# Other places and other turns for the sums of w1's blocks in a fused HGRN2 and mixer kernel

## The chip, the cores and the metric

The kernel runs on one core of a Trainium2 chip. The metric is device time in microseconds (us) for one execution, and the median of several executions stands for a kernel. Times within an execution come from one profiled execution and are counted from the start of its span. The engines are called as the profile calls them: PE is TensorE, DVE is VectorE, ACT is ScalarE, POOL is GpSimd, SP is SyncE.

## The reference, cut to what matters

Two blocks follow each other. The first is a gated recurrence for each of 4 batches and 8 heads, over 768 steps, with a state of 48 x 48. Its output, with the heads side by side, is the input `x` of the second, a mixer: a low-rank mixing along the sequence, and a two-layer channel network with a residual.

```python
# q, k, v, f_logit: (4, 8, 768, 48)
f = 1.0 / (1.0 + np.exp(-f_logit))
for t in range(S):
    state = f[:, :, t, :, None] * state + np.einsum('bhd,bhe->bhde', k[:, :, t], v[:, :, t])
    y[:, :, t] = np.einsum('bhd,bhde->bhe', q[:, :, t], state)
# x: (4, 768, 384), the heads of y side by side
# U: (768, 32), V: (32, 768), w_ch1: (384, 1536), w_ch2: (1536, 384)
h = xt @ U @ V                      # xt = x.transpose(0, 2, 1)
u = x + h.transpose(0, 2, 1)
ch = np.maximum(u @ w_ch1, 0.0) @ w_ch2
return u + ch
```

## The kernel before

**Attention.** The sequence is cut into chunks of 64 steps, and two heads are handled together; such a pair is a unit, and there are 16 units, 4 for each batch. The gates' products within a chunk are scanned on VectorE (`keep`, L827, backwards, into row 4 of the tile `late`; `read`, L845, forwards, into row 5). For a unit TensorE then makes the scores `sc` (L923), the transposed keys `pt` (L950), the chunks' states `ds` (L971), and the output `y` in two parts: from the states (L1009) and from the masked scores (L1027). VectorE multiplies `sc` by the causal mask into `A` (L936) and scans the states into `added` (L993); GpSimd copies them into `st` (L997), which the first part of `y` reads. ScalarE copies `ds` into `added` (L978), `pt` into `kb` (L954) and `y` into `x` (L1033), and spreads the chunks' whole gates into `whole` (L960).

**Mixer.** For each batch, `low_rank`, `added_up` and `mix` (`ph`, `pu`) add the mixing to `x`; `turn` transposes it into `uT` (`put`); `first` multiplies by `w1` (`pz`, L279) with a relu on ScalarE into `z_all` (L314); and the second layer is done by `seven` in four steps of `pw` products (L365), with sums `S` of z blocks (tiles `w_raw`, four additions of `sums_of`). A sequence block `a` is 256 rows; a batch has three. The tile `z_all` has 18 columns of 256 and is used as three thirds of 6 columns.

**The last blocks.** From batch 2's second block on, the first layer is done by `fewer` with 15 products of 128 x 512 instead of the plain ones (`pp`, L468). For that it needs sums of blocks of `x` (`sums_of_x`) and 14 sums of blocks of `w1`, 128 x 512 each. `W_SUMS` lists these: `(9, 0, '+', 1)` makes node 9 from nodes 0 and 1; nodes below 9 are blocks of `w1` itself. `w_node` looks up where a node lies, through `W_PLACES`, an index into the list `w_places`: ten pieces of `late` (0 to 9), the two tiles `fz` (10 and 11), and `added` (12). Those tiles serve the attention too, so a sum can be written only when attention no longer needs its place. `places_of_x` lists the places of the x sums: three `v_nat` tiles and two `st` tiles, of four pieces each, in that order.

**Order of the work.** The order on TensorE is the order of the program. In the second half of the kernel VectorE and ScalarE get theirs from a scheduler by priority; operations in `add` and the mask have a high one. `steps` yields the attention's pieces, `attention` runs them, and `Fill` puts the mixer's products between them. The 14 sums are called from `beside` in the last stretch of attention (the units of batch 3, beside block 0 of batch 2's mixer): one after each piece from piece 16 on.

```python
pieces = beside(steps((B - 1) * HP + 1, NU + 1), 10 * (HP - 2) - 4, [lambda i=i: sum_of_w(i) for i in range(len(W_SUMS))])
todo = m.first(0) + m.ready(0) + m.halved(0)
attention(pieces, Fill(todo[:-1], 33))
```

Just ahead of it stands `start_mixer(2, after)`: the mixing of batch 2 between the four steps of `seven` for batch 1's last block.

Of the kernel before, what the change touches and what calls it, by code (L numbers as in the profile page):

```python
# [39 lines left out]
W_SUMS = (  # L40
    (9, 0, '+', 1), (10, 4, '+', 9), (11, 5, '-', 10), (12, 2, '+', 11), (13, 4, '-', 5), (14, 4, '+', 7),
    (15, 6, '+', 14), (16, 5, '-', 15), (17, 8, '+', 16), (18, 6, '+', 17), (19, 3, '+', 15), (20, 0, '-', 18),
    (21, 0, '+', 14), (22, 2, '+', 20),
)
W_PLACES = (0, 1, 2, 3, 4, 5, 6, 7, 8, 9, 10, 11, 5, 12)
PRODUCTS = (
    ((2, 17),), ((7, 18),), ((11, 20),), ((6, 21),), ((13, 0),), ((1, 3),), ((8, 15),), ((4, 19),),
    ((9, 10),), ((10, 16),), ((3, 22),), ((12, 11),), ((0, 12),), ((15, 13),), ((14, 9),),
# [489 lines left out]
def factored_path(ctx, tc, q, k, v, f_logit, moe_U, moe_V, moe_w_ch1, moe_w_ch2, out, ok):  # L538
# [5 lines left out]
    B, H, S, D = q.shape  # L544
    P = nc.NUM_PARTITIONS
    C = P // 2
    NCH = S // C

    NBL = S // P
    HP = H // 2  # L550
# [4 lines left out]
    NFC = FF // P  # L555
    NU = B * HP
# [25 lines left out]
    z_all = const.tile([P, 3 * NFC // 2, 2 * P], F32, name="z_all")  # L582
# [20 lines left out]
    def load(n, *names):  # L603

        b, hp = divmod(n, HP)
        for nm in names:
            if nm == "v":
                v_tiles[n] = three.tile([P, NBL, 2, D], F32, name="v_nat")
            for par in range(2):
                head = src[nm][b, 2 * hp + par]  # L610
                if nm in "kq" and n < HP:
                    if par == 0:
                        nc.sync.dma_start(
                            out=packed(n, nm).rearrange("p (h t) -> p h t", h=2),
                            in_=src[nm][b, 2 * hp : 2 * hp + 2].rearrange("h (p c) d -> p h (c d)", p=P),
                        )
                    continue
                if nm == "v" and par:

                    for s in range(2):  # L620
                        nc.sync.dma_start(
                            out=v_tiles[n][(1 - s) * C : (2 - s) * C, :, par, :],
                            in_=head.rearrange("(c s p) d -> s p c d", s=2, p=C)[s],
                        )
                    continue
                if nm == "v" or n < TURNED:
                    dst = v_tiles[n] if nm == "v" else nat[n % 2][nm]
                    nc.sync.dma_start(out=dst[:, :, par, 0:D], in_=head.rearrange("(c p) d -> p c d", p=P))
                    continue
                head = head.rearrange("(c i) d -> i c d", i=NB)  # L630
                for part in range(2):
                    p0 = par * PAD + part * NB
                    n_ch = min(NB, D - part * NB)
                    nc.sync.dma_start(
                        out=raw[n % 2][nm][p0 : p0 + NB, :].rearrange("p (c d) -> p c d", d=NB)[:, :, 0:n_ch],
                        in_=head[:, :, part * NB : part * NB + n_ch],
                    )
# [225 lines left out]
    FG = FF // 3  # L863
    w_places, x_places, v_places, room = [], [], [], {}

    def w_node(n):
        if n < 9:
            return w1[:, n // 3, n % 3 * FG : (n % 3 + 1) * FG]
        return w_places[W_PLACES[n - 9]]

    def sum_of_w(i):
        if i == 0:
            flat = late.rearrange("p a s -> p (a s)")
            w_places.extend(flat[:, j * FG : (j + 1) * FG] for j in range(7 * S // FG))
            w_places.extend(t[:, 0:FG] for t in fz + [added])
            assert max(W_PLACES) < len(w_places)
        n, p, sign, q = W_SUMS[i]
        nc.vector.tensor_tensor(w_node(n), w_node(p), w_node(q), ALU.add if sign == "+" else ALU.subtract)

    def places_of_x():  # L880
        if not x_places:
            some = [three.tile([P, NBL, 2, D], F32, name="v_nat").rearrange("p c h d -> p (c h d)") for _ in range(3)]
            some += [two.tile([P, NCH, D], F32, name="st").rearrange("p c d -> p (c d)") for _ in range(2)]
            x_places.extend(t[:, i * P : (i + 1) * P] for t in some for i in range(NCH * D // P))
        return x_places

    def places_of_values():
# [155 lines left out]
    def front(n, *names):  # L1043

        if n >= NU:
            return []
        if n not in ahead:
            names_of = ("gates", "keep", "keys", "read_back", "queries", "gates_end", "unpack_k", "unpack_q")
            ahead[n] = dict(zip(names_of, prepare(n)))
        return [ahead[n].pop(nm) for nm in names if nm in ahead[n]]  # L1050

    def rear(n, *names):

        if not 0 <= n < NU:
            return []
        if n not in here:
            here[n] = dict(zip(("kept", "states", "scan", "scores", "read", "inner", "mask", "spread"), attend(n)))
        return [here[n].pop(nm) for nm in names if nm in here[n]]

    def joined(*groups):  # L1060

        groups = [g for g in groups if g]
        for _ in groups[1:]:
            yield lambda: None
        if groups:
            yield lambda: [f() for g in groups for f in g]

    def steps(first, last):

        def behind(n):  # L1070

            return HP + 3 <= n < NU - 1

        for n in range(first, last):
            if n < NU:
                yield from joined(rear(n - 2, "inner"), rear(n - 1, "scores"), rear(n, "kept"))
            else:
                for piece in rear(n - 2, "inner") + rear(n - 1, "scores"):
                    yield lambda: None
                    yield piece  # L1080
            if behind(n):
                yield from front(n, "read_back", "queries")
            if n + 1 < NU and n + 1 not in v_tiles:
                load(n + 1, "v")
            yield from front(n + 1, "gates", "keep", "keys")
            yield from joined(rear(n - 1, "read"), rear(n, "states", "scan"))
            if not behind(n + 1):
                yield from front(n + 1, "read_back", "queries")
            if n + 1 == last:
                yield from rear(n - 1, "inner")  # L1090
                if n + 2 < NU:
                    load(n + 2, "v")
# [5 lines left out]
            piece()  # L1098
        fill.rest()

    def beside(pieces, n, calls):

        for i, piece in enumerate(pieces):
            yield piece
            for f in calls[:1] if i >= n else []:
                calls.remove(f)
                f()
        assert not calls

    def start_mixer(b, after, early=(), late=()):  # L1110
# [13 lines left out]
    with tc.manual_schedule(engines={nc.vector.engine, nc.scalar.engine}):  # L1124
# [18 lines left out]
        done, rest = slice(0, 2 * (HP - 1) * D), slice(2 * (HP - 1) * D, DM)  # L1143
# [10 lines left out]
        for n in range(HP):  # L1154
            last = n + 1 == HP
            pieces = rear(n - 1, "scan") + front(n, "unpack_q", "keys") + rear(n, "spread") + rear(n - 1, "read")
# [79 lines left out]
        n = len(m.seconds) // (NBL // 2)  # L1236
# [3 lines left out]
        n = 2 * HP + 2  # L1240
# [3 lines left out]
        pieces, fill = steps(n - 1, 3 * HP + 1), Fill(m.main, 10 * HP - 3)  # L1244
# [3 lines left out]
    for b in range(2, B - 1):  # L1248
        if b > 2:
            pieces, fill = steps(b * HP + 1, (b + 1) * HP + 1), Fill(m.main, 10 * HP)  # L1250
        after = m.after
        attention(pieces, fill)
        m = start_mixer(b, after)

    pieces = beside(steps((B - 1) * HP + 1, NU + 1), 10 * (HP - 2) - 4, [lambda i=i: sum_of_w(i) for i in range(len(W_SUMS))])
    todo = m.first(0) + m.ready(0) + m.halved(0)
    attention(pieces, Fill(todo[:-1], 33))

# [315 lines left out]
@with_exitstack  # L1574
def kernel(
    ctx: ExitStack,
    tc: tile.TileContext,
    q: bass.AP,
    k: bass.AP,
    v: bass.AP,  # L1580
    f_logit: bass.AP,
    moe_U: bass.AP,
    moe_V: bass.AP,
    moe_w_ch1: bass.AP,
    moe_w_ch2: bass.AP,
    out: bass.AP,
):


    nc = tc.nc  # L1590
    args = (q, k, v, f_logit, moe_U, moe_V, moe_w_ch1, moe_w_ch2, out)
    flag = ctx.enter_context(tc.tile_pool(name="flag", bufs=1))
    ok = flag.tile([1, 1], I32, name="ok")
    with ExitStack() as inner:
        factored_path(inner, tc, *args, ok)
    good = nc.values_load(ok[0:1, 0:1], min_val=0, max_val=1)
    with tc.If(good == 0):
        with ExitStack() as inner:
            general_path(inner, tc, *args)
# [30 lines left out]
```

## Time and profile before

| what | value |
|---|---|
| median of 3 executions | 473.09 us (471.94 to 474.18) |
| the profiled execution's own time | 474.62 us |
| its span, first to last instruction | 472.9 us |
| mean granted TensorE clock | 0.994 |
| PE busy | 458.5 us (97% of the span) |
| DVE busy | 351.3 us (74%) |
| ACT busy | 165.9 us (35%) |
| POOL busy | 54.3 us (11%) |
| the 14 sums of w1's blocks (L878) | first at 240.0 us, last at 315.2 us |

In the lines of the profile, a group or a timeline row gives the engine, the line of the kernel, the operation, output and inputs by the program's names, and the shape; a timeline row begins with its start and its duration, and ends, in brackets, with the time for which the engine had been idle and what ended that. Matrix products of 32-bit numbers are recorded twice each, so `x12` is six instructions of the program. A wait that the view calls "issue" has no releaser that it can name.

### The profile page before, as it was taken

Reading aid. Unit: us, or ns where it says so; the run is one execution under the profiler, and the core shown is the slowest. Engines: PE = TensorE matmul, PEld = TensorE weight load, DVE = VectorE, ACT = ScalarE, POOL = GpSimd, SP = SyncE. Lnnn points to the kernel's source line nnn. Section 1 sums busy time; section 2 is a strip of 40 time slices with the busy share of each in tenths; the row PEclk is TensorE's granted clock in tenths of the full one; section 3 lists DMA queues with packets and bytes.
Section 4 is the critical chain, followed back from the end, with each engine's and each line's share of the span. In section 5 each row is a group of like instructions: output and inputs, shape, how many; then the busy total and the mean of one; then the engine's idle time right before and its main releaser. Section 6 shows DMA issues by size and latency. Waiting matters only on the chain.

```text
span 472.9 us, 13003 instructions
## 1 busy us (share of the span) xinstructions
PE 458.5 (97%) x5639; PEld 396.7 (84%) x5639; DVE 351.3 (74%) x579; ACT 165.9 (35%) x315; POOL 54.3 (11%) x60
## 2 busy tenths in 40 slices
PE   8989999999999999999999999989999999999995
PEld 5876888876666588998898888989979999999994
DVE  5767789979998687685575459977796877859632
ACT  5775776562332144222313134311312312112200
POOL 2002445634112001010101001110000000000000
PEclk9999999999999999999999999989999999999998
DMA  9948987677678414406334021000000000000001
GB/s 197 200 110 200 223 215 180 151 113 109 117 116 136 75 26 57 64 19 102 43 69 77 0 51 28 3 3 19 18 1 1 35 1 34 1 14 22 2 35 40
DMA packets 148313, 34.36 MB, mean 73 GB/s; under 512 B 136790, under 2 KB 146710, under 8 KB 148246
## 3 DMA queue, kind: packets, MB, share of 16 engines
q1 hardware_dynamic: 148246, 33.44, 36.1%
q8 instruction: 46, 0.75, 0.6%
q14 instruction: 21, 0.17, 0.1%
HBM read 28.70 MB, written 4.72 MB: 71 GB/s over the span
## 4 chain that ended last, share of the span: by engine, by line
PE 84%; DVE 7%; ACT 3%; issue 2%; DMA 2%; SPq 1%; DVEq 0%; ACTq 0%
PE pw L365 27%; PE pz L279 23%; PE pp L468 12%; PE po L331 5%; PE y L1009 2%; PE y L1027 2%; PE sc L923 2%; PE ds L971 2%; PE pt L744 2%; PE pt L790 1%; PE pt L950 1%; DMA v_nat<-in_v_dram 1%; PE pu L214 1%; PE put L267 1%; PE idle L1131 1%
## 5 line engine op out<-in xcount | busy, mean ns | idle before, releaser
L279 PE MATMUL pz<-uT,w 128*128 128x256 f32 x492 | 111.5, 382 | 0.3
L279 PEld LDWEIGHTS pz<-uT,w 128*128 128x128 f32 x492 | 91.7, 190 | 12.9 <-ACT uT L268 0.6
L997 POOL COPY st<-added 128x576 f32<-128x576 f32 x12 | 18.2, 1516 | 189.2 <-DVE added L993 189.2
L365 PE MATMUL pw<-zw,w_raw 128*128 128x192 f32 x216 | 39.2, 336 | 0.0
L365 PE MATMUL pw<-w,z_all 128*128 128x192 f32 x216 | 37.3, 327 | 0.0
L365 PEld LDWEIGHTS pw<-zw,w_raw 128*128 128x128 f32 x216 | 36.3, 195 | 0.6 <-issue 0.3
L101 POOL TENSOR_TENSOR w<-w_y,w_r 128x384 int32<-128x384 int32 x24 | 31.5, 1314 | 39.5 <-DVE w_y L100 25.0
L314 ACT ACTIVATE z_all<-pz 128x512 f32<-128x512 f32 x33 | 19.6, 598 | 46.4 <-PE pz L279 46.0
L365 PEld LDWEIGHTS pw<-w,z_all 128*128 128x128 f32 x216 | 35.3, 190 | 0.5
L468 PE MATMUL pp<-v_nat,late 128*128 128x128 f32 x224 | 28.8, 275 | 0.0
L468 PEld LDWEIGHTS pp<-v_nat,late 128*128 128x128 f32 x224 | 27.0, 192 | 0.0
L827 DVE TENSOR_TENSOR_SCAN late<-fz,late 128x768 f32<-128x768 f32 x12 | 21.1, 1755 | 7.2 <-ACT fz L822 7.1
L461 ACT ACTIVATE other<-other 128x512 f32<-128x512 f32 x18 | 11.3, 631 | 40.3 <-DVE other L204 40.3
L331 PE MATMUL po<-w,zw 128*128 128x384 f32 x72 | 25.2, 495 | 0.0
L331 PE MATMUL po<-w,z_all 128*128 128x384 f32 x72 | 24.7, 493 | 0.0
L936 DVE TENSOR_TENSOR A<-sc,causal 128x768 f32<-128x768 f32 x16 | 15.2, 952 | 10.6 <-PE sc L923 10.6
L331 PEld LDWEIGHTS po<-w,zw 128*128 128x128 f32 x72 | 13.2, 190 | 9.6 <-issue 0.8
L845 DVE TENSOR_TENSOR_SCAN late<-fz,other 128x768 f32<-128x768 f32 x12 | 21.0, 1750 | 0.2
L331 PEld LDWEIGHTS po<-w,z_all 128*128 128x128 f32 x72 | 13.3, 190 | 8.9 <-DVE o L204 0.6
L978 ACT COPY added<-ds 48x576 f32<-48x576 f32 (+1 forms) x28 | 17.8, 635 | 6.8 <-PE ds L971 6.3
L461 ACT ACTIVATE z_all<-z_all 128x512 f32<-128x512 f32 x12 | 7.6, 630 | 33.3 <-DVE z_all L204 33.3
L98 DVE TENSOR_SCALAR w_y<-w_y 128x384 f32<-128x384 f32 (+3 forms) x27 | 12.2, 451 | 8.8 <-ACT w_y L91 8.7
(219 smaller groups left out, 846.6 us busy)
## 6 DMA issues: line engine op xcount, KB each, us to landing
w_raw<-in_moe_w_ch_dram SPq DMA_DIRECT2D x18, 384.0 KB, 3.8
out_dram<-o SPq DMA_DIRECT2D x24, 192.0 KB, 2.0
v_nat<-in_v_dram SPq DMA_DIRECT2D x16, 144.0 KB, 3.9
v_nat<-in_v_dram SPq DMA_DIRECT2D x32, 72.0 KB, 4.0
zw<-in_moe_w_ch_dram SPq DMA_DIRECT2D x6, 384.0 KB, 5.6
w<-in_k_dram SPq DMA_DIRECT2D x4, 288.0 KB, 3.9
w<-in_q_dram SPq DMA_DIRECT2D x4, 288.0 KB, 4.7
late<-in_f_logit_dram SPq DMA_DIRECT2D x10, 96.0 KB, 2.7
```

Of the source, the lines that this page charges most:

```text
L101: nc.gpsimd.tensor_tensor(dst.bitcast(I32), shaped(y.bitcast(I32)), shaped(r), ALU.add)
L279: nc.tensor.matmul(pm[:, i * 2 * P : (i + 1) * 2 * P], lhsT=w1[:, m, o : o + P], rhs=uT[a][:, m, :], start=(m == 0), stop=(m == NDC - 1))
L314: nc.scalar.activation(z[a, c][:, k : k + 2, :].rearrange("p i t -> p (i t)"), pm, AF.Relu)
L331: nc.tensor.matmul(pm, lhsT=z[a, i // NI][:, i % NI, s * P : (s + 1) * P], rhs=w2[:, i, :], start=(i == 0), stop=(i == NFC - 1))
L365: nc.tensor.matmul(W["pm"][:, n * HM : (n + 1) * HM], lhsT=lhs[:, i, :], rhs=rhs[:, i, :], start=(i == 0), stop=(i == NI - 1))
L461: nc.scalar.activation(dst, dst, AF.Relu, scale=float(SIGNS[n]))
L468: nc.tensor.matmul(pm[:, i, r * P : (r + 1) * P], lhsT=room["w"](wn)[:, r * P : (r + 1) * P], rhs=x_node(a, xn), start=((xn, wn) == of[0]) ...
L827: nc.vector.tensor_tensor_scan(backwards(X, S - 1, S), backwards(f, S, S), backwards(ends, S - 1, S), 0.0, ALU.mult, ALU.add,)
L845: nc.vector.tensor_tensor_scan(Y, f[:, 0:S], starts, 0.0, ALU.mult, ALU.add)
L936: nc.vector.tensor_tensor(T["A"], sc[:, :, 0 : NBL * C].rearrange("p h (c i) -> p h c i", i=C), causal.unsqueeze(1).unsqueeze(1).broadcast ...
L978: nc.scalar.copy(added[r, 1:].rearrange("p (e c s) -> p e c s", c=NBL, s=2), ds[r, :, 0 : NBL * D].rearrange("p s (c e) -> p e c s", e=D),)
L997: nc.gpsimd.tensor_copy(st, states.rearrange(by_e, c=NCH))
```

## The change

`W_PLACES` gives the nodes other places: the first three lie in the last third of `z_all`, which joins the list as places 13 to 15, and `added` and two pieces of `late` are no longer used. The first three sums are called before the last stretch of attention, right after `start_mixer`. The others have turns: sum 3 after piece 5 of that stretch, then after pieces 7, 8 and 13 to 20. `places_of_x` puts two pieces of its first `v_nat` tile first, then the second tile's, then the rest.

```diff
-W_PLACES = (0, 1, 2, 3, 4, 5, 6, 7, 8, 9, 10, 11, 5, 12)
+W_PLACES = (13, 14, 15, 0, 1, 2, 10, 3, 9, 5, 4, 6, 2, 11)
...
             w_places.extend(t[:, 0:FG] for t in fz + [added])
+            flat = z_all[:, NFC:, :].rearrange("p i t -> p (i t)")
+            w_places.extend(flat[:, j * FG : (j + 1) * FG] for j in range(3))
             assert max(W_PLACES) < len(w_places)
...
-            x_places.extend(t[:, i * P : (i + 1) * P] for t in some for i in range(NCH * D // P))
+            t2, t1, t3, *rest = [[t[:, i * P : (i + 1) * P] for i in range(NCH * D // P)] for t in some]
+            x_places.extend(t2[:2] + t1 + t2[2:] + t3 + [p for t in rest for p in t])
...
-    def beside(pieces, n, calls):
+    def beside(pieces, calls):
 
         for i, piece in enumerate(pieces):
             yield piece
-            for f in calls[:1] if i >= n else []:
-                calls.remove(f)
-                f()
+            while calls and calls[0][0] <= i:
+                calls.pop(0)[1]()
...
-    pieces = beside(steps((B - 1) * HP + 1, NU + 1), 10 * (HP - 2) - 4, [lambda i=i: sum_of_w(i) for i in range(len(W_SUMS))])
+    turns = 5, 7, 8, 13, 14, 15, 16, 17, 18, 19, 20
+    early_sums = len(W_SUMS) - len(turns)
+    for i in range(early_sums):
+        sum_of_w(i)
+    pieces = beside(steps((B - 1) * HP + 1, NU + 1),
+                    [(t, lambda i=i: sum_of_w(i)) for i, t in enumerate(turns, early_sums)])
```

## The prediction, made before the changed kernel was run

> **What bounds the kernel now.** I read the page first, for the engine that fills the span.
>
> ```profile
> PE 458.5 (97%) x5639; PEld 396.7 (84%) x5639; DVE 351.3 (74%) x579; ACT 165.9 (35%) x315; POOL 54.3 (11%) x60
> PEclk9999999999999999999999999989999999999998
> PE 84%; DVE 7%; ACT 3%; issue 2%; DMA 2%; SPq 1%; DVEq 0%; ACTq 0%
> ```
>
> TensorE is busy in 97% of the span and carries 84% of the chain of waits, so VectorE's 74% costs only where TensorE waits for it. The clock row has one dip inside the span, the slice from 307.4 to 319.2 us. The 14 sums that the change moves run on VectorE from 240 to 316 us, so I read the timeline there. It shows the one long hole of TensorE:
>
> ```profile
> 303.87 0.89 PE L923 MATMUL sc<-qT,kz 48*64 48x64 f32 x48
> 305.21 2.22 PE L365 MATMUL pw<-zw,w_raw 128*128 128x192 f32 x12
> 307.36 0.90 PE L1009 MATMUL y<-st,qT 48*64 48x48 f32 x44
> 309.87 1.14 PE L971 MATMUL ds<-v_nat,kb 64*48 64x48 f32 x48 [1.60 <-issue]
> 310.94 3.42 PE L365 MATMUL pw<-zw,w_raw 128*128 128x192 f32 x12
> 315.13 2.22 PE L365 MATMUL pw<-w,z_all 128*128 128x192 f32 x12
> ```
>
> `ds` waits 1.60 us, which the view calls "issue" since it names no releaser. In the built program `ds` waits for the mask `A<-sc` (L936): it reuses the PSUM buffer that the mask reads. After the hole, twelve `pw` take 3.42 us where equal groups take 2.22: the granted clock is 0.63 from 311.0 to 314.3, and the trace's clock record holds 0.5 for 3.41 us from 310.0. VectorE's timeline says why the mask was late:
>
> ```profile
> 302.74 1.35 DVE L993 TENSOR_TENSOR_SCAN added<-added,whole 128x576 f32<-128x576 f32 x1
> 304.01 0.93 DVE L764 TENSOR_TENSOR qT<-qT,late 128x768 f32<-128x768 f32 x1
> 304.97 1.58 DVE L878 TENSOR_TENSOR late<-w,late 128x512 f32<-128x512 f32 x1
> 306.75 0.68 DVE L878 TENSOR_TENSOR late<-w,late 128x512 f32<-128x512 f32 x1
> 308.02 0.68 DVE L878 TENSOR_TENSOR late<-w,late 128x512 f32<-128x512 f32 x1
> 308.82 0.94 DVE L936 TENSOR_TENSOR A<-sc,causal 128x768 f32<-128x768 f32 x1
> 304.22 1.79 POOL L997 COPY st<-added 128x576 f32<-128x576 f32 x1 [9.99 <-DVE added L993]
> ```
>
> `sc` was done at 304.76, but three sums (L878) stood ahead of its mask. The first took 1.58 us instead of 0.68, beside GpSimd's copy of `st`. The mask ended at 309.76 and `ds` began at 309.87.
>
> [...] that copy takes 1.21 us undisturbed, 1.79 behind the multiplication of 304.01, and 2.54 at 149.68 behind a scan; the sum at 304.97 then ends 0.54 us after the copy. [...]
>
> **The change, part by part.** The sums stay 14 instructions of the same shape; none is added on TensorE, ScalarE, GpSimd or SP, and no DMA is moved. VectorE's queue in the built programs shows where they go. Before: 1 at 240 us, 8 between the mask at 280.29 and `S1` (`w_raw<-z_all`, 298.40), 5 from 304.97 to 315.25. After: 4 in the mixing of batch 2 (three in the last third of `z_all`), 10 between that mask and `S1`, none later.
>
> (a) *Four sums in the mixing.* They stand between `w_y<-w_y,x` and `o<-o,pw`:
>
> ```profile
> 267.72 0.35 DVE L204 TENSOR_TENSOR w_y<-w_y,x 128x192 f32<-128x192 f32 x1
> 271.01 0.56 DVE L204 TENSOR_TENSOR o<-o,pw 128x384 f32<-128x384 f32 x1 [2.94 <-PE pw L365]
> ```
>
> VectorE is idle there for 2.94 us. The first three wait for TensorE's `pw<-w,z_all` group (266.91 to 269.02), the last reader of that third, in steps of two matmuls: about 267.8, 268.5 and 269.1. From 268.0, with 0.73 us between dependent sums (295.93 to 296.66), they end at 268.0 + 3 x 0.73 + 0.68 = 270.9, before 271.01. Cost 0. Queued behind them are `o<-o,pw` and the three `x<-x,pu`, for which the next `pw` and the transposes wait: 0.1 us of slack.
>
> (b) *Two sums more before `S1`.* Independent neighbours start 0.60 us apart (333.00 to 333.61), so 2 x 0.60 = 1.2 us, less VectorE's 0.45 us of idleness ahead of `S1`: everything from there is 0.75 us later. The scan L993 starts at 303.49 and ends at 304.84, the multiplication at 305.67; GpSimd's copy waits for it and ends at 306.75. The `y` group needs the copy at 307.36: 0.6 us spare. `S2` ends at 301.8, needed at 305.21. In this stretch ScalarE's `whole` also moves ahead of one relu; that relu ends near 293.5 and its `pz` buffer is wanted at 295.1. Cost 0.
>
> (c) *Five sums gone from 304 to 316.* ScalarE's `whole` and `w_y` follow the scan, so VectorE's `w_y<-x,pw` starts at 305.95, `o` at 306.35, and two small `v_nat` sums wait for GpSimd until 306.75. The mask comes at 307.1 and ends at 308.05. TensorE is in `y` until 308.28, so `ds` does not wait: 309.87 - 308.29 = **1.58 us** less.
>
> (d) *The clock.* At half clock `ds` took 1.14 us instead of about 0.57, and the `pw` group 3.35 instead of 2.15 (chain of waits): 0.57 + 1.20 = **1.77**; half of 3.41 is 1.7, which I use. [...]
>
> (e) *Order of the x sums' places* (`t2[:2] + t1 ...`): the first two x sums still need the oldest `v_nat` buffer, the next ones a later one. In the built order they stand after `w_y`, ahead of the mask of 318.27, where VectorE waited 0.79 us and had lost the 0.69 us sum at 315.25. Cost 0.
>
> (f) From 321.8 on the order of work is the same, and both TensorE (to 333) and VectorE's chain (333 to 348.6) start from what precedes them, so what is won at 308 reaches the end.
>
> **Sum.** The profiled execution takes 474.62 us, of which 472.9 is span and 1.72 lies around it; it stands 1.53 us above the median of 473.09, which is nearly the clock dip, and the runs spread from 471.94 to 474.18. Against its own time the change is worth -1.58 - 1.7 = -3.3, giving 471.3. Against the median I count the dip half: -1.58 - 0.85 = -2.4, giving **470.7 us**. Both ends stand: 473.09 - 3.3 = 469.8 if most runs have the dip, 473.09 - 1.58 = 471.5 if few have.
>
> **What the trace does not show** is a queue of VectorE instructions with two SBUF inputs and no wait between them beside a waiting GpSimd copy. After, a sum and the scan L845 follow the scan L993 at about 292. If GpSimd gets in between, L845 starts 1.2 us later (a copy); if not, GpSimd waits until about 295, and `st` is needed at 297.66. I take the second, at no cost; the first is the next case.
>
> **The rivals.**
> 1. *The wait passes to `st` (0.22).* With the 1.2 us all is 1.95 later, not 0.75: the scan ends at 306.0, the copy at 307.9, `y` starts 0.6 late, the mask ends at 309.2 and `ds` starts at 309.3. Only 0.6 of the 1.58 is won, and with half the dip 473.09 - 0.6 - 0.85 = 471.6. For it: the copy did get between two such instructions at 304.8. Against: there the sum had a wait of its own.
> 2. *No gain (0.12).* As 1, but the dip comes all the same from the two shorter holes, or before's runs mostly lack it: 472.5 to 473.1.
> 3. *The early sums hold the mixing (0.11), slower.* If the three in `z_all` wait for the whole `pw` stage, to 270.9, and not for their own blocks' readers, `o<-o,pw` and the `x` additions come 4 x 0.68 = 2.7 us late. TensorE's next `pw` waits for the first `x` addition (0.60 us already at 272.88), and the hole brings a dip: +2.7 + 1.7 - 2.0 won later = 475.5. It decides once the first sum starts after about 268.2. Against it: the waits in the built program name the three readers.
>
> **How the numbers follow.** The forecast has 0.55: faster by over 0.5% (under 470.72; 0.5% is about what a measurement of this kernel can tell from no change) in 0.41 of it, as it lies on that border and the dip decides. Rival 1 adds 0.05 faster and 0.17 same, rival 2 0.12 same, rival 3 0.11 slower. Faster 0.46, same 0.43, slower 0.11. The range runs from 468.9 (all of the dip and some 0.9 for a hole of the unprofiled runs that I do not see) to 473.3 (rival 2), leaving out rival 3 and little else.
>
> **What would show it.** Right: four L880 sums between 268 and 271, no idle time ahead of `ds` (then line L974) near 308, no half clock after it, and `pp` starting about 318.5 instead of 321.9. Rival 1: a scan L845 of about 2.9 us near 293 and idle time of `y` for `st`. Rival 3: idle time of `pw` or the transposes near 273. The prediction is wrong if `ds` still waits for the mask, or if the stretch from 322 to the end changes its length.

## The result, and the profile after

The changed kernel takes **471.78 us** (median of 22 executions, 470.56 to 473.57), the kernel before 473.29 us on the same chip (22 executions); the ratio is 0.9964, 95% interval 0.9953 to 0.9975. That is 1.5 us or 0.36% less, inside the 0.5% that the prediction called no difference. The profiled execution takes 471.81 us with a span of 470.0 us and a mean granted clock of 0.998.

These are the rows of the page of the changed kernel for busy time, clock and the chain of waits:

```profile
PE 456.2 (97%) x5639; PEld 394.9 (84%) x5639; DVE 352.3 (75%) x579; ACT 165.6 (35%) x315; POOL 54.2 (12%) x60
...
PEclk9999999999999999999999999999999999999999
...
PE 75%; DVE 13%; issue 3%; ACT 3%; DMA 2%; SPq 2%; POOL 0%; DVEq 0%; ACTq 0%; POOLq 0%
```

TensorE is busy for 2.3 us less with as many instructions, mostly since no products run at half clock near 310: the clock row has no dip left, and the granted clock is 1.00 from 304 to 322, where before it was 0.50 from 310 to 313. VectorE is busy for 1.0 us more, also with as many instructions, and has 13% of the chain where it had 7%. The chain of before ran over TensorE from 276 to 308 us; now a stretch of it, from about 280 to 306, runs over VectorE and ends at GpSimd's copy of `st`, for which TensorE waits. So something on VectorE there sets the time.

TensorE's timeline of the changed kernel (start, duration, work; in brackets the idle time ahead and what ended it):

```profile
272.67 2.22 PE L365 MATMUL pw<-w,w_raw 128*128 128x192 f32 x12
...
303.66 0.89 PE L926 MATMUL sc<-qT,kz 48*64 48x64 f32 x48
...
305.00 2.22 PE L365 MATMUL pw<-zw,w_raw 128*128 128x192 f32 x12
...
307.54 0.90 PE L1012 MATMUL y<-st,qT 48*64 48x48 f32 x44 [0.31 <-POOL st L1000]
...
308.80 0.76 PE L974 MATMUL ds<-v_nat,kb 64*48 64x48 f32 x48 [0.37 <-ACT seen L1019]
309.49 2.22 PE L365 MATMUL pw<-zw,w_raw 128*128 128x192 f32 x12
...
319.16 0.27 PE L1301 MATMUL lp<-ident,low 128*1 128x128 f32 x1
319.27 1.05 PE L468 MATMUL pp<-uT,late 128*128 128x128 f32 x8
```

The one hole of 1.60 us is now two short ones, 0.31 us of `y` for `st` and 0.37 us of `ds`. The view names `seen` for the second, but `seen` was done at 308.64; the mask ended at 308.70 and `ds` began at 308.80, as close behind it as in the kernel before (309.76 and 309.87), so it is the mask still. The `pw` group after `ds` takes 2.22 us, not 3.42. `lp`, a single product ahead of the first `pp`, starts at 319.16.

VectorE's and GpSimd's timeline of the changed kernel says why `st` came late:

```profile
267.78 0.69 DVE L880 TENSOR_TENSOR z_all<-w 128x512 f32<-128x512 f32 x1
268.57 1.49 DVE L880 TENSOR_TENSOR z_all<-w,z_all 128x512 f32<-128x512 f32 x2
...
270.10 0.69 DVE L880 TENSOR_TENSOR late<-w,z_all 128x512 f32<-128x512 f32 x1
...
270.81 0.55 DVE L204 TENSOR_TENSOR o<-o,pw 128x384 f32<-128x384 f32 x1
...
290.56 1.35 DVE L996 TENSOR_TENSOR_SCAN added<-added,whole 128x576 f32<-128x576 f32 x1
...
291.83 0.67 DVE L880 TENSOR_TENSOR late<-w,late 128x512 f32<-128x512 f32 x1
...
292.05 1.52 POOL L1000 COPY st<-added 128x576 f32<-128x576 f32 x1 [35.49 <-DVE added L996]
...
292.42 2.77 DVE L845 TENSOR_TENSOR_SCAN late<-fz,other 128x768 f32<-128x768 f32 x1
...
299.88 0.95 DVE L204 TENSOR_TENSOR w_raw<-z_all 128x768 f32<-128x768 f32 x1
...
304.21 1.35 DVE L996 TENSOR_TENSOR_SCAN added<-added,whole 128x576 f32<-128x576 f32 x1
...
305.70 1.78 POOL L1000 COPY st<-added 128x576 f32<-128x576 f32 x1 [12.13 <-DVE added L996]
...
307.76 0.94 DVE L939 TENSOR_TENSOR A<-sc,causal 128x768 f32<-128x768 f32 x1
```

Four sums lie in the mixing, and `o<-o,pw` follows them without a pause. At 292 GpSimd's copy of `st` goes in between a sum and the scan L845, and the scan takes 2.77 us instead of 1.75: it ends at 295.19, which is 1.62 us after the copy's end at 293.57. From there what follows on VectorE is about 1.0 us later than it need be (experiment 1 shows this): `S1` (299.88), the scan of the states (304.21), the copy of `st` (until 307.48) and the mask.

### The profile page after: what moved, and what is told of

Same layout as the page of the kernel before. It is cut to its first block, busy times and chain, and to the rows that moved or that the text cites. A ratio compares the mean times of both kernels' runs of the same rounds, so it can differ in the third digit from the quotient of the medians.

```text
span 470.0 us, 13005 instructions
## 1 busy us (share of the span) xinstructions
PE 456.2 (97%) x5639; PEld 394.9 (84%) x5639; DVE 352.3 (75%) x579; ACT 165.6 (35%) x315; POOL 54.2 (12%) x60
## 4 chain that ended last, share of the span: by engine, by line
PE 75%; DVE 13%; issue 3%; ACT 3%; DMA 2%; SPq 2%; POOL 0%; DVEq 0%; ACTq 0%; POOLq 0%
PE pw L365 25%; PE pz L279 18%; PE pp L468 12%; PE po L331 5%; PE y L1012 2%; PE y L1030 2%; PE ds L974 1%; PE sc L926 1%; PE pt L744 1%; PE pt L790 1%; SPq L634 1%; PE pu L214 1%; DVE late L845 1%; DMA v_nat<-in_v_dram 1%; DVE kz L721 1%
## 5 line engine op out<-in xcount | busy, mean ns | idle before, releaser
L365 PE MATMUL pw<-zw,w_raw 128*128 128x192 f32 x216 | 38.0, 329 | 0.0
L365 PEld LDWEIGHTS pw<-zw,w_raw 128*128 128x128 f32 x216 | 35.1, 190 | 0.6 <-issue 0.3
L845 DVE TENSOR_TENSOR_SCAN late<-fz,other 128x768 f32<-128x768 f32 x12 | 22.0, 1834 | 0.2
L468 PE MATMUL pp<-v_nat,late 128*128 128x128 f32 x152 | 19.1, 275 | 0.0
L1012 PEld LDWEIGHTS y<-st,qT 48*64 48x64 f32 x704 | 13.6, 137 | 6.4 <-issue 3.9
```

The lines of the kernel that those rows point to most:

```text
L365: nc.tensor.matmul(W["pm"][:, n * HM : (n + 1) * HM], lhsT=lhs[:, i, :], rhs=rhs[:, i, :], start=(i == 0), stop=(i == NI - 1))
L468: nc.tensor.matmul(pm[:, i, r * P : (r + 1) * P], lhsT=room["w"](wn)[:, r * P : (r + 1) * P], rhs=x_node(a, xn), start=((xn, wn) == of[0]) ...
L845: nc.vector.tensor_tensor_scan(Y, f[:, 0:S], starts, 0.0, ALU.mult, ALU.add)
L1012: nc.tensor.matmul(o(c % 2, par, c // 2), lhsT=T["q"][rows[par], chunk[c]], rhs=T["st"][rows[par], c, :], start=(c <= 2), stop=False, skip ...
```

## The experiments

The kernel before ran beside every kernel: 473.15 us on the chip of the first four, 473.84 on that of the next four, 473.33 on that of 9 to 11, and 473.24 beside the last. Two theories were tried; both can hold at once. **Port** (a name only: the runs show how long the two instructions take, not what in the chip keeps them apart): what the change won at 308 is partly lost because the copy of `st` holds the scan L845 at 292. **Clock**: the gain is in part the half-clock stretch behind the hole, which comes only in some executions. I count an execution with a mean granted clock of 0.995 or less as one with such a dip, for 3.41 us at half clock take 0.0036 off the mean. The mean does not say where the dip lies.

**1. The copy of `st` of unit 13 on ScalarE**, in the changed kernel.

```diff
-                    nc.gpsimd.tensor_copy(st, states.rearrange(by_e, c=NCH))
+                    (nc.scalar.copy if n == NU - 3 else nc.gpsimd.tensor_copy)(st, states.rearrange(by_e, c=NCH))
```

> The changed kernel, with one of GpSimd's twelve copies of st (the one near 292 us) done by ScalarE. Port theory (GpSimd's copy holds up the scan L845): L845 takes 1.75 us there instead of 2.77, all that follows on VectorE up to the mask is about 1 us earlier, y no longer waits for st near 307 (0.31 us), ds no longer for what stands ahead of it near 308.8 (0.37), and pp starts some 0.7 us earlier than in the changed kernel; median about 471.1. Rival, that the two sums more ahead of S1 alone make VectorE late: L845 is long or not, the waits of y and ds stay, median 471.8 as the changed kernel.

Measured: 470.99 us (10 executions), ratio 0.9929 (0.9907 to 0.995). It ran once more beside the changed kernel (7 and 8 below). In that second trace ScalarE, VectorE and TensorE read:

```profile
293.11 1.22 ACT L1000 COPY st<-added 128x576 f32<-128x576 f32 x1 [3.25 <-DVE added L996]
293.58 1.75 DVE L845 TENSOR_TENSOR_SCAN late<-fz,other 128x768 f32<-128x768 f32 x1
...
300.03 0.95 DVE L204 TENSOR_TENSOR w_raw<-z_all 128x768 f32<-128x768 f32 x1
...
307.91 0.95 DVE L939 TENSOR_TENSOR A<-sc,causal 128x768 f32<-128x768 f32 x1
308.31 0.84 PE L1012 MATMUL y<-st,qT 48*64 48x48 f32 x42
...
308.96 0.25 PE L974 MATMUL ds<-v_nat,kb 64*48 64x48 f32 x2
```

The scan runs beside the copy in its usual 1.75 us. This trace lies 1.16 us behind that of the changed kernel at 267, so `S1` at 300.03 is 1.0 us earlier there, and neither `y` nor `ds` waits. For the delay and the two waits the port theory holds; what they are worth in time is taken up under 7 and 8.

**2. The same for unit 14 in the kernel before**, where the copy stretched a sum to 1.58 us.

```diff
-                    nc.gpsimd.tensor_copy(st, states.rearrange(by_e, c=NCH))
+                    (nc.scalar.copy if n == NU - 2 else nc.gpsimd.tensor_copy)(st, states.rearrange(by_e, c=NCH))
```

> The kernel before, with the one copy of st near 304 us done by ScalarE. Port theory: the sum at 305 takes 0.68 us instead of 1.58; ScalarE's whole and w_y come some 0.6 us later, so the mask comes about 0.6 us earlier and the wait of ds falls from 1.6 to about 1.0 us; median 472.4 to 472.8. Rival, that the sums' number alone counts: the sum keeps 1.58 us or ds keeps its 1.6 us of waiting, median 473.3.

Measured: 473.50 us, ratio 1.0 (0.9982 to 1.0017): a miss. From its timeline:

```profile
305.14 1.25 ACT L997 COPY st<-added 128x576 f32<-128x576 f32 x1 [3.60 <-DVE added L993]
...
305.99 0.69 DVE L878 TENSOR_TENSOR late<-w,late 128x512 f32<-128x512 f32 x1
...
310.73 0.76 PE L971 MATMUL ds<-v_nat,kb 64*48 64x48 f32 x48 [1.45 <-issue]
```

The stretch is gone, 0.69 us instead of 1.58. But ScalarE has `whole` and `w_y` to copy next, and with 1.25 us for `st` ahead of them VectorE had to wait 0.65 us for `w_y`; the wait of `ds` fell by 0.15 us only. In these two places the remedy took the wait away where ScalarE had room and not where it had none.

**3. The hole of the kernel before filled** with six products that nothing reads.

```diff
...
+            if n == NU - 1:
+                for _ in range(6):
+                    nc.tensor.matmul(mixer_now[0].W["pm"][:, DM:512], lhsT=ident, rhs=ident, start=True, stop=True)
             ds = ps_big.tile([P, 2, 512], F32, name="ds", tag="big")
...
```

> The kernel before, with six products of 128 x 128 on TensorE ahead of ds in the last unit, into unused columns (about 1.4 us of work whose result nobody reads): they fill the hole in which ds waits for the mask. Clock theory: ds starts as late as before, but the half clock of 3.41 us does not come near 310 in any run; what the median gains is 1.7 us times the share of runs of before that have the dip, 0.3 to 0.9 us, so 472.4 to 473.0. Rival, that the dip has another cause or is rare: median 473.3 and, if there is a dip in the profile, at the same place.

Measured: 473.26 us, ratio 1.0 (0.9983 to 1.0017). Its timeline has the hole filled and the next `pw` at full clock:

```profile
309.68 1.60 PE L967 MATMUL pw<-ident 128*128 128x128 f32 x12
...
311.36 0.76 PE L974 MATMUL ds<-v_nat,kb 64*48 64x48 f32 x48
312.04 2.22 PE L365 MATMUL pw<-zw,w_raw 128*128 128x192 f32 x12
```

Executions with a dip became 5 of 22 (29 of 63 for the kernel before on this chip), but the median did not move, where 472.4 to 473.0 had been expected. The direction of the count fits the clock theory, but 5 of 22 is too few to tell from 29 of 63 with confidence.

**4. The old order of the x sums' places** in the changed kernel.

```diff
-            t2, t1, t3, *rest = [[t[:, i * P : (i + 1) * P] for i in range(NCH * D // P)] for t in some]
-            x_places.extend(t2[:2] + t1 + t2[2:] + t3 + [p for t in rest for p in t])
+            x_places.extend(t[:, i * P : (i + 1) * P] for t in some for i in range(NCH * D // P))
```

> The changed kernel with the x sums' places in the order of before (that part of the change undone). Prediction's part (e): no effect, median 471.8 within 0.3, the same waits of y and ds. Rival, that the new order frees VectorE ahead of the masks at 307 and 315: masks 0.3 to 0.6 us later, median 472.2 or more.

Measured: 472.97 us, ratio 0.9984 (0.9968 to 1.0), so most of the gain is gone: without the new order the new places and turns are 0.2 us ahead of the kernel before, at the edge of what the interval can show. The timeline:

```profile
307.46 0.62 DVE L204 TENSOR_TENSOR v_nat<-uT,v_nat 128x128 f32<-128x128 f32 x2
308.00 0.95 DVE L938 TENSOR_TENSOR A<-sc,causal 128x768 f32<-128x768 f32 x1
309.05 0.75 PE L973 MATMUL ds<-v_nat,kb 64*48 64x48 f32 x48 [1.02 <-ACT seen L1018]
```

Two more x sums stand ahead of the mask, and `ds` waits 1.02 us instead of 0.37. The new order alone, in the kernel before, was not run; whether it would bring the gain without the new places is open.

**5. The places and the x order alone**, in the kernel before, with its calls (one after each piece from piece 16 on) as they were.

```diff
-W_PLACES = (0, 1, 2, 3, 4, 5, 6, 7, 8, 9, 10, 11, 5, 12)
+W_PLACES = (13, 14, 15, 0, 1, 2, 10, 3, 9, 5, 4, 6, 2, 11)
...
+            w_places.extend(flat[:, j * FG : (j + 1) * FG] for j in range(3))
...
+            x_places.extend(t2[:2] + t1 + t2[2:] + t3 + [p for t in rest for p in t])
```

> The kernel before with two parts of the change alone: the new W_PLACES (with the last third of z_all in the list) and the new order of the x sums' places. The 14 calls stay as before, one after each piece from piece 16 on. Theory 'places decide': a sum can be put as early as its place is free and the scheduler does so, whatever piece calls it; four sums again lie in the mixing (near 268 to 271 us), none between the scan of 304 and the last mask, y and ds wait about 0.3 to 0.4 us each near 308, and the time is that of the changed kernel, 471.8 us (471.3 to 472.3). Theory 'turns carry it': the sums stay behind the mask of 280 or behind the scan near 304, ds still waits 1.3 us or more near 308, and the time is 473.0 to 473.5.

Measured: 471.81 us, ratio 0.9959 (0.9942 to 0.9977), as the changed kernel. Four sums lie in the mixing all the same (268.32 to 271.31). So the scheduler put these sums as early as their places were free; the new turns and the early calls move nothing that counts. Here L845 runs ahead of the scan of the states, in 1.75 us, and the copy falls between two sums:

```profile
293.67 1.52 POOL L1000 COPY st<-added 128x576 f32<-128x576 f32 x1 [36.58 <-DVE added L996]
294.03 1.71 DVE L880 TENSOR_TENSOR late<-w,fz 128x512 f32<-128x512 f32 x1
```

The second of the two pays 1.03 us (1.71 against 0.68): for the scan and for the addition the price is the same. `y` and `ds` wait 0.36 us each.

**6. The turns alone**: the changed kernel with the old `W_PLACES`.

```diff
-W_PLACES = (13, 14, 15, 0, 1, 2, 10, 3, 9, 5, 4, 6, 2, 11)
+W_PLACES = (0, 1, 2, 3, 4, 5, 6, 7, 8, 9, 10, 11, 5, 12)
```

> The changed kernel with the old W_PLACES: the calls and the order of the x sums' places are the new ones, the sums' places are the old. Theory 'places decide': no sum gets into the mixing; five go ahead of the mask of the last unit but one near 297 us, whose products ds then wait (more than 1 us near 298), and S1 and what follows come later, so nothing is won: 472.8 to 474.5 us. Theory 'turns carry it': the sums spread out as in the changed kernel, no wait over 0.5 us near 298 or 308, and 471.3 to 472.3.

Measured: 1476.13 us. The kernel tests the smallest product of gates and, where that fails, computes everything anew by a second program; the trace shows that program from 470.6 us on. The likely reason, argued and not shown, is this: in program order the early sums now stand ahead of attention's last writes to those pieces of `late`, so that each spoils what the other needs. So these turns can't be had with the old places, and the time tells nothing of their worth. The first 470 us do show the expected order, with no sum in the mixing and five ahead of the mask of 298.13, and then the waits:

```profile
310.27 0.90 PE L1012 MATMUL y<-st,qT 48*64 48x48 f32 x44 [1.56 <-POOL st L1000]
...
312.97 0.95 PE L974 MATMUL ds<-v_nat,kb 64*48 64x48 f32 x48 [1.80 <-issue]
```

Behind these two waits the granted clock of this trace is 0.50 from 314 to 316 us, as behind the hole of the kernel before.

**7 and 8. The changed kernel, and the kernel of 1, beside each other.** No edit but that of 1.

> The changed kernel itself, so that the next one is compared with it on one chip: 471.8 us (471.4 to 472.2), mean clock at or above 0.996 in nine runs of ten.

> The changed kernel with the copy of st for unit 13 (n = NU - 3) on ScalarE, again, beside the changed kernel. Port theory: the scan L845 near 293 takes 1.75 us and not 2.77, y and ds wait for nothing near 308, and the time is 0.7 us under the changed kernel's on this chip (0.5 to 1.0), by the 0.31 + 0.37 us of waits that go. Rival: the two waits are made up elsewhere and the two are within 0.3 us.

Measured: 471.93 us, ratio 0.997 (0.9952 to 0.9988), with 4 of 22 executions at a clock of 0.995 or less, where two had been expected; and 471.47 us, ratio 0.9953 (0.9936 to 0.9969). The version with the copy on ScalarE is 0.46 us ahead in the medians, slightly under the expected 0.5 to 1.0, and the two intervals overlap, so this pair alone does not show the gain in time. In all, four runs with that edit (1 and 8, and 10 and 12 with more masks) took 470.99 to 471.47 us, and the two of the changed kernel 471.78 and 471.93.

**9. The early sums done twice** in the changed kernel: what rival 3 would cost.

```diff
     for i in range(early_sums):
         sum_of_w(i)
+        sum_of_w(i)
```

> The changed kernel with each of the three early sums done twice (same output), the price of rival 3 measured: of the seven sums, five stand ahead of the o addition, one between it and the first x addition, one between the x additions. So the first x addition starts about 273.1 us and not 271.66, and the pw group behind it (272.67) waits 2.0 us and not 0.6. Theory 'no slack there': nothing later gives it back, 1.4 us more by the trace, and a hole of 2.0 us brings a dip of the clock in about half of the runs, so 473.3 to 474.3 us in the median. Theory 'slack': the wait is given back by later waits (those of y and ds near 308, 0.7 us in all) and the time is 471.8 to 472.6.

Measured: 473.26 us, ratio 0.9998 (0.9977 to 1.0018). The timeline:

```profile
271.93 0.68 DVE L880 TENSOR_TENSOR z_all<-w,z_all 128x512 f32<-128x512 f32 x1
272.15 0.92 PE L214 MATMUL pu<-h,V 32*128 32x384 f32 x4 [0.76 <-DVE w_y L204]
...
273.53 2.22 PE L365 MATMUL pw<-w,w_raw 128*128 128x192 f32 x12 [0.46 <-DVE x L204]
...
320.13 1.05 PE L468 MATMUL pp<-uT,late 128*128 128x128 f32 x8
```

In the changed kernel the sums end 0.02 us ahead of `o<-o,pw`. Three more on VectorE there cost TensorE 1.1 us: the products `pp` start at 320.13 instead of 319.27, in a trace that is 0.23 us ahead at 266. The waits near 308 stay at 0.32 and 0.36 us. Nothing gives it back, and the change's gain is gone. The wait fell in two parts, though, not in one of 2.0 us, and only 2 of 14 executions had a dip.

**10 to 12. The hole put back.** The mask three times instead of once, in the kernel of 1, and in 11 the products of 3 too. In 10 and 11 I had the wrong unit: the mask of the last one is that of 316.8 us, not that of 308; 12 has `NU - 2` in the line below, and no products.

```diff
-            if b:
+            for _ in range(3 if n == NU - 1 else 1 if b else 0):
                 mask()
```

> The changed kernel with unit 13's copy of st on ScalarE (which waits for nothing near 308) and with the last unit's mask done three times instead of once (same output): ds has to wait for the third, 1.3 to 1.6 us. Clock theory: a hole of this length alone brings back the dips, a mean clock of 0.995 or less in 40 to 60 of 100 runs (kernel before: 46 and 51 of 100; without a hole 10 to 25), and the median is 472.4 to 473.2 us. Rival: the dips of the kernel before come from elsewhere, the share stays at 10 to 25 of 100, and the median is that of the kernel without the hole, 471.0 to 471.5, plus the wait, less what is given back later: 472.0 to 472.6. The shares tell the two apart better than the medians.

> As the last one, with six products of ident by ident into an unused part of a PSUM tile ahead of the last unit's ds, so that TensorE computes while ds waits. Clock theory: as many microseconds of waiting for the mask, but no hole in TensorE's work and so no dip there: a mean clock of 0.995 or less in 10 to 25 of 100 runs, median 0.2 to 0.8 us under that of the one before. Rival: the same share and the same median as the one before, within 0.2 us.

> The hole, now at its place: the changed kernel with unit 13's copy of st on ScalarE, and the mask of unit 14 (n = NU - 2, the one near 308 us) done three times instead of once (same output), which ds near 309 has to wait for: by the trace of the kernel without it 1.5 to 1.8 us of TensorE's idleness, as long as that of the kernel before (1.58). Clock theory: a hole of this length brings the dips back, a mean clock of 0.995 or less in 40 to 60 of 100 runs (kernel before so far: 75 of 165; this kernel without the hole: 6 of 46), and with the wait the median is 472.6 to 473.5 us. Rival: the dips of the kernel before come from elsewhere: 5 to 20 of 100 runs, and 472.3 to 472.8 us.

Measured: 471.08 us (0.9949, 0.9929 to 0.9968), 472.97 us (0.9979, 0.9966 to 0.9993) and 471.25 us (0.9944, 0.9924 to 0.9964). In 10 nothing waits near 308 and `y` waits 0.33 us near 320. In 11 the six products, 1.60 us where `ds` would not have waited, cost 1.9 us in the medians against 10 on the same chip: what is put on TensorE at 308 reaches the end. In 12 the mask is the right one, and still there is no hole:

```profile
309.23 0.82 ACT L957 COPY kb<-pt 128x768 f32<-128x768 f32 x1
...
309.96 2.93 DVE L939 TENSOR_TENSOR A<-sc,causal 128x768 f32<-128x768 f32 x3
...
311.00 0.24 PE L974 MATMUL ds<-v_nat,kb 64*48 64x48 f32 x2
```

`ds` begins 1.89 us ahead of the masks' end. In the built program it has been given the PSUM buffer of `pt`, read last by `kb`, and not, as in the kernel before, that of `sc`; the likely reason is that the pool hands out the buffer whose last reader comes first in the scheduled order. So the wait of `ds` for the mask in the kernel before was one for a buffer, not for data. Giving `ds` the buffer of `pt` in the kernel before was not tried.

## Why the prediction was right or wrong, point by point

The change is a gain, as forecast, and inside the range, but the range was wide enough for every case save rival 3. The likeliest case (470.7 us) did not come. The first rival did, by both of its signs: a scan L845 of 2.77 us and a wait of `y` for `st`. That its 471.6 us meets the 471.78 measured is partly luck: it put 0.6 us on the waits and 0.85 on the clock, where 0.92 and, by the counts below, about 0.54 came. `ds` still waits for the mask, which the prediction had named as the sign of being wrong, but for 0.37 us and not 1.60.

- **The failed step is the choice in "what the trace does not show".** I let the sum and the scan L845 run through ahead of the copy, at no cost. GpSimd went in between, and L845 lost 1.02 us. Experiment 1 takes that away and both waits near 308 go; experiment 5 shows the loss on another instruction. L845 ends 1.62 us after the copy, nearly its own 1.75 us, and the second sum of experiment 5 ends 0.55 us after its copy, of its own 0.68: by these times the later of the two did little before the earlier had ended. Which of the two goes next, the trace of before had left open; in the changed kernel, 4, 5, 7 and 9 it was the copy.
- **(a) right.** Four sums in the mixing at no cost; experiment 9 gives the price of more. Rival 3 did not come, but a delay there would have cost time: 1.1 us by the trace for three sums more.
- **(b) mis-sized.** `S1` came 1.48 us later by the timeline, 1.69 after allowing for the 0.21 us by which this trace is ahead at 267, not 0.75; the difference is about L845's 1.02. So `st` was late by 0.31 us, where 0.6 us to spare were forecast.
- **(c) mis-sized.** Of the 1.60 us of `ds`, 0.68 stays in two waits; 0.92 was won, not 1.58. The first rival had 0.6. The sign for being right, `pp` at about 318.5, came at 319.27.
- **(d) the dip at 310 is gone, its size and its cause open.** That a dip goes with a hole, here and in rival 3, and that half of the executions have it, was the forecast's estimate, made from one trace in which a dip of 3.41 us lies behind a hole of 1.60. In the trace it was worth 1.6 us and not 1.77: at full clock `ds` takes 0.76 us, not 0.57 (1.14 before), and the `pw` group 2.22 instead of 3.42. In all runs beside the experiments, 81 of 182 executions of the kernel before had a clock of 0.995 or less, near the half that was estimated; of the changed kernel 5 of 44 (1 of 22, then 4 of 22). With about 1.6 us for each (474.57 against 472.91 us in the medians with and without, on the first chip) that is (0.45 - 0.11) x 1.6 = 0.54 us in the mean, not 0.85, as some dips come from elsewhere: the profiled execution of 1 has a mean clock of 0.995, yet its `pw` groups from 305.89 and 309.41 take 2.22 us each, and that of 12 has 0.989, with 0.91 in the first 40 us, 0.96 from 430 on and 1.00 between. Together with 0.92 it makes 1.46 us, and 1.51 was measured. That the hole causes the dips is not shown: five runs without a hole near 308 (1, 8, 10, 11, 12) had 8 of 80, and one with 1.45 us (2) had 7 of 22, but the filled hole had 5 of 22, two kernels with short waits (4 and 5) had 4 of 20 and 6 of 22, and the hole put back never came about. In the kept traces a half clock followed the 1.60 us of before and the 1.56 and 1.80 us of 6, and none the 1.45 us of 2 or the 1.02 us of 4, where the next `pw` group took 2.22 us; that is one execution each. Executions without a dip also gained more (472.91 to 473.07 us before, 471.58 to 471.78 after) than the 0.92 us of waits, so the split between the two terms is loose.
- **(e) wrong.** The order of the x places was costed at nothing, from their position ahead of a later mask. Ahead of the mask of 308 it is worth 0.65 us of waiting, and 1.1 us in the medians (472.97 in experiment 4, 471.8 to 471.9 with the new order); the difference of the two is unexplained. Part (c) had read the built order, with two x sums ahead of that mask and not four, so the gain stood in the sum, but was credited to the five sums of `w1`'s blocks alone.
- **(f) right.** From the start of `lp`, just ahead of `pp`, to the end it is 150.8 us after and 151.1 before, and experiment 11 shows that the path has no slack there. In the kernel before `lp` reads:

```profile
321.81 0.27 PE L1294 MATMUL lp<-ident,low 128*1 128x128 f32 x1
```

The spans of the two profiled executions differ by 472.9 - 470.0 = 2.9 us: 0.21 us ahead of 267, about 0.9 of waits, 1.6 of clock, and 0.25 behind the start of `lp`.

## What to carry to other kernels

When VectorE's work is moved, look at what GpSimd waits for at the place that it moves to: a copy may slip in between two instructions, and the second pays for it (about 1.0 us here). In a kernel whose order a scheduler makes, the calls' turns may be without effect while a free place or another buffer decides; undo the parts one by one before crediting them. And before making a slow engine faster for a wait that has no releaser in the view, see whether it is for data or only for a buffer, which another may replace.

## What the runs showed of the hardware that was not expected

- Between two VectorE instructions with two SBUF inputs each and no wait between them, a waiting GpSimd copy got in: the second instruction took 2.77 us instead of 1.75 (scan) and 1.71 instead of 0.68 (addition). The copy itself took 1.52 us instead of 1.21, behind the first of the two.
- The price went with what came next. In the kernel before, the copy of that unit took 1.53 us, also behind a sum, but the next instruction was the mask, which has one input in SBUF and one in PSUM. It took its usual 0.95 us, so nothing was lost:

```profile
292.48 0.67 DVE L878 TENSOR_TENSOR late<-w 128x512 f32<-128x512 f32 x1
...
292.70 1.53 POOL L997 COPY st<-added 128x576 f32<-128x576 f32 x1 [35.93 <-DVE added L993]
...
293.07 0.95 DVE L936 TENSOR_TENSOR A<-sc,causal 128x768 f32<-128x768 f32 x1
```

- The same copy on ScalarE took 1.22 us (8) and 1.25 us (2), and the VectorE scan beside it in 8 took its 1.75 us.
